# Rounding converted weights on GpSimd, with a shorter warm-up and a new instruction order, in attention with a feed-forward block

## The chip, the core and the metric

The kernel runs on one core of a Trainium2 chip. The metric is the device time of one execution in microseconds (us). The core has five engines with one instruction queue each: TensorE (PE; its weight loads are shown as PEld), VectorE (DVE), ScalarE (ACT), GpSimd (POOL) and SyncE (SP, which here only starts transfers). Instructions of one queue start in order; an instruction waits until those of other engines that it depends on have signalled.

## What is computed

Eight batches of eight heads; queries are averaged in pairs, so 1152 keys meet 576 queries of 64 dimensions. Attention's result goes through a feed-forward block whose hidden value is the largest of three products. All in 32-bit floats.

```python
q_pool = q.reshape(B, H, S // 2, 2, D).mean(axis=3)
scores = scale * np.matmul(q_pool, k.transpose(0, 1, 3, 2))
scores = scores - np.max(scores, axis=-1, keepdims=True)
attn = np.exp(scores)
attn = attn / (np.sum(attn, axis=-1, keepdims=True) + 1e-09)
x = np.matmul(attn, v)            # then heads side by side: 4608 tokens x 512
h = np.maximum(np.maximum(x @ w1, x @ w2), x @ w3)   # 512 -> 768
return h @ w_out                                     # 768 -> 512
```

## The kernel before

**Units.** The work is cut into 64 units: a batch (8), a pair of heads (4), one half of the queries (288). Unit d computes scores for nine blocks of 128 keys (`scores`, lines 570 to 770) and the values (`values`, lines 773 to 981). Each score block is a product of rounded keys with the high and the low half of the queries (L592, L593, tile pqk, two buffers); ScalarE copies it out of PSUM (L605, tile s), VectorE keeps a running maximum (L611, L614, tile acc). The maximum over keys is spread (L646 to L688) and subtracted (L739: on VectorE, for one head of the first 8 units on GpSimd), ScalarE takes exponentials (L745), GpSimd or TensorE adds over keys (ksum L762, L764; psum L870), and TensorE multiplies by the values (pav L786). A score tile is free again only when the value product and the key sum of the unit have read it.

**Two halves of a number.** TensorE is fed with rounded numbers (F32R). So a 32-bit operand is split: the high half is the rounded copy, the low half the difference. Queries and keys are split that way (heads after the first: L473, L477, L480, L484), x (L942, L945), the hidden value h (L1151, L1154) and the weights.

**The first pair of heads** has code of its own (`first_heads`, lines 363 to 442). Its keys come in three blocks c of 384 columns per head; ScalarE rounds a block (L402) and VectorE (block 0) or GpSimd (blocks 1 and 2) makes the low half (L407). While the first transfers run, TensorE is kept busy by a warm-up of products on ones: 6 steps of 1920 columns, 36 matmuls of 288 columns (L350, list WARM).

**The weights.** They arrive as 64-bit floats. For batch 0, `convert` (lines 993 to 1029) turns 512 columns at a time into 32-bit floats: ScalarE scales both words (L1004, L1012), VectorE shifts (L1007), GpSimd adds (L1015). `piece` (lines 1031 to 1050) then makes the two halves, in 26 pieces: the high one on ScalarE (L1042), the low one on GpSimd (L1045). `store` writes the finished group of weights (tile w, two buffers, 13 groups) to memory (L1057); batches 1 to 7 only read it back (`fetch`, L1083). The feed-forward products are L1123 (tile ph, three weight matrices) and L1177 (tile po, w_out); their results leave PSUM by ScalarE or VectorE (hm L1141, L1143; ob L1193). They have two PSUM buffers ("ff"). Batch b's feed-forward runs beside the attention units of batch b + 1, the last one alone.

**The order.** Every step names the engines that it may run on with a cost in us, and the steps that it waits for. `arrange` (lines 151 to 244) simulates the engines by these costs and takes, on the engine that is free first, the ready step of the lowest rank; the order that results is written out as it is, queue by queue. A step's rank is mostly its class's entry in RANK (lines 35 to 83; "first_" entries are added for units below 8, ffn, rate and their "0" forms shift feed-forward steps by batch and by place in the batch), plus an entry of TUNE (18 per class, for units 0 to 17). From unit 18 on TUNE gives nothing. Ranks are in the thousands and unit numbers only below 64, so classes stand in the order of their RANK:

```python
return Step(plan, lambda: d + R[ffn] + R[rate] * n * i / 576 + R[key] + tuned(key, d + 8 * i / 576), engines, fn, after, **kw)
```

Here n is 8 and i runs from 0 to 576 within a batch's feed-forward; i is 432 where w_out begins.

Of the kernel before, what the change touches and what calls it, by code (L numbers as in the profile page):

```python
# [22 lines left out]
QH = 288  # L23
# [12 lines left out]
    "qk": -3130.6658,  # L36
    "cp": -1826.0788,
    "mx": -3810.9001,
    "rows": -8627.0757,
    "red": -43.3158,  # L40
    "bc": -3872.8251,
    "sub": 6258.0329,
    "spread": 1085.8561,
    "exp": 2331.9394,
    "keys": 2364.6864,
    "av": -1042.0366,
    "xcopy": -3440.4973,
    "psum": 3883.7886,
    "sums": -2422.2708,
    "inv": 2073.6634,  # L50
    "xm": -7068.4991,
    "load": -380.5043,
    "prep": 2642.0348,
    "move": 4629.5675,
    "split": 2839.5003,
    "ffn": 3762.7022,
    "ffn0": -465.7092,
    "rate": 35.7318,
    "mm": 2092.8736,
    "fetch": -2282.852,  # L60
    "evac": -3702.58,
    "hhigh": -1168.7886,
    "hlow": -5067.5631,
    "conv": -1572.4688,
    "rate0": 690.1207,
    "first_qk": -4407.8227,
    "first_cp": -1651.3185,
    "first_mx": -1346.0576,
    "first_sub": -2911.0325,
    "first_exp": -3297.3165,  # L70
    "first_keys": -289.0476,
    "first_av": 2482.2468,
    "first_xcopy": -3190.556,
    "first_psum": -1205.5463,
    "first_sums": -2967.258,
    "away": 2349.2695,
    "first_inv": 1449.6935,
    "first_xm": 6167.6523,
    "first_load": 2699.3536,
    "first_prep": -2816.0705,  # L80
    "first_move": 5356.3819,
    "first_split": 50.1713,
# [6 lines left out]
    "rows": [-175.81, -2924.97, -2232.22, -1314.67, 460.97, -3131.21, -418.16, -775.77, 2638.05, -927.09, 854.38, -786.06, 870.99, 708.38, -1156.9, 783.78, -1226.45, -1786.97],  # L89
    "red": [-2241.91, -542.05, 2974.71, 1758.28, -503.57, -1328.97, -782.7, 268.29, -512.53, 1720.33, -786.63, 1917.46, -1276.72, -581.32, 1526.87, -982.28, 184.37, -1249.52],  # L90
    "bc": [-664.57, 172.69, 2235.21, -9.63, -2441.8, -729.01, -812.33, 1298.95, -879.37, 2407.08, -662.96, 602.59, -2313.96, -5.85, -833.79, -753.42, 1381.1, 1053.26],
    "sub": [1288.35, -514.25, -1250.29, 867.55, -2087.59, 292.93, 318.27, -1814.19, 1210.45, 2668.87, 2171.77, 369.02, -1898.63, 935.45, -1626.68, -3948.77, 760.75, 1293.88],
    "spread": [-3017.17, -782.21, 146.5, -2338.72, 283.85, 375.19, 1264.03, -184.45, 2476.42, -589.85, -889.16, -2121.58, -406, -365.93, -385, 222.06, 1726.42, -33.34],
    "exp": [-1955.85, 4048.31, 465.95, -1397.74, 2172.54, 57.59, 651.46, 1134.86, -2438.63, 651.63, 813.75, -394.37, -1502.34, -93.57, 128.48, -687.9, -1912.66, -882.69],
    "keys": [1293.35, 536.44, -1206.73, -2762.49, 299.9, -744.66, -1425.81, -1312.24, 2139, -1917.58, -1157.75, 956.01, -1910.32, 1738.77, 1666.71, -1147.47, 1393.11, 254.81],
    "av": [-46.8, -2772.09, 336.08, 254.7, -2006.33, 1355.89, -3050.17, 1140.74, 218.38, -1842.44, 1293.07, 1165.55, 1669.17, -2607.14, -3030.98, -265.36, 1892.55, -473.41],
    "xcopy": [1417.03, 3211.46, -2262.39, 1303.49, 1208.8, -1718.5, -1526.9, -1467.75, 1451.2, -291.98, -438.62, 1058.33, 24.62, -517.18, 2377.34, -1577.76, 1437.68, 1053.33],
    "psum": [-2696.17, 1357.23, 1123.89, -4598.94, -144.12, 2609.44, -634.47, -2662.38, 1500.72, 1846.17, 111.17, -1242.53, -742.72, 989.9, 116.69, 160.62, -1251.54, 5420.26],
    "sums": [755.08, -874.34, 2205.9, 1188.61, 2102.95, 1489.15, 888.5, 2924.58, -884.62, 329.82, 2011.77, 1627.77, -2594.78, 42.45, -415.63, 733.21, 998.28, 1272.22],
    "inv": [463.45, 1.26, -506.82, 1133.91, -722.58, 827.13, 992.35, 5572.02, 3655.18, -2791.21, 1439.12, -1477.71, -3129.81, 262.16, 1885.92, -1076, 735.07, 1310.17],  # L100
    "xm": [250.61, 363.42, 1361.26, -1104.64, 147.92, -2589.27, 2273.74, 1215.79, 575.43, -427.34, -352.49, -2255.54, -399.51, 1677.21, -584.59, -1147.25, -244.86, -131.38],
    "load": [2580.7, -865.03, -2039.98, -671.65, -1758.9, 899.44, -899.78, -2532.24, 591.45, -1279.02, -1811.66, -1149.59, -471.31, -2359.87, 747.59, 1478.6, 781.71, 3443.62],
    "prep": [476.96, 26, 434.64, 281.83, -1092.64, -1322.6, 197.4, 1715.5, -1576.39, -2069.68, 777.66, 2379.06, 2668.96, 973.44, -514.25, -545.63, 217.96, 1502.65],
    "move": [-2126.63, 2238.79, 2678.63, 569.66, 1278.92, -1444.12, -2083.36, 1728.83, 846.71, -399.4, -501.92, 120.68, -383.26, 2378.59, 559.61, 1007.33, -1306.78, -1660.5],
    "split": [-1015.88, -1480.7, 1498.66, -186.59, 1691.42, -889.06, 512.38, -1694.37, -1338.11, 333.89, -1295.44, -2899.8, -2636.37, 4383.83, 550.6, -2444.64, 241.3, 116.47],
    "mm": [-115.23, 683.46, 280.54, 2090.93, -498.08, -510.9, 1188.76, 1536.93, 1257.07, 486.25, 402.45, -1117.45, -2060.38, -1143.13, 652.06, -1654.27, 259.36, -1950.85],
# [27 lines left out]
WARM = [288] * 6  # L134
APART = 0
SWITCH = 0.3
WIRE = 0.4


class Step:  # L140
    def __init__(self, plan, urgency, engines, fn, after, tail=0.0, take=None, give=None, cols=0, mode=0, size=0):
        self.size = size
        self.urgency, self.engines, self.fn = urgency, engines, fn
        self.tail, self.take, self.give, self.cols, self.mode = tail, take, give, cols, mode
        self.index = len(plan)
        self.after = [a for a in after if a is not None]
# [100 lines left out]
def pe(n):  # L247
    return ("pe", n * 1e-3)
# [15 lines left out]
def tile_attention_ffn(  # L264
# [11 lines left out]
    nc = tc.nc  # L276
# [75 lines left out]
    x = None  # L352
# [634 lines left out]
    def ffn(b, cs, d):  # L987
# [117 lines left out]
        n = 0  # L1105
# [163 lines left out]
```

## Time and profile before

| | us |
|---|---|
| median of 3 runs | 1326.4 (1324.9 to 1326.55) |
| profiled execution, its own time | 1328.54 |
| span of that execution, first to last instruction | 1326.8 |
| TensorE busy | 1292.6 (97%) |
| VectorE busy | 996.9 (75%) |
| ScalarE busy | 985.3 (74%) |
| GpSimd busy | 1054.7 (79%) |
| mean granted clock of TensorE | 0.987 of full |

How to read it: busy times add up the instructions of an engine and overlap with those of others. TensorE's matmuls are pipelined and the ends of their records are modelled, so a matmul of 288 columns has a record of about 0.3 us while one starts every 0.13 us; a TensorE that looks busy may still have small gaps. The chain of waits is the one path of work that ended last, followed back from the end: at each step to what released it. What is on the chain set the time; what is not was hidden. A releaser is inferred from signals.

### The profile page before, as it was taken

The numbers are of one execution on the slowest core, as the hardware profiler recorded it, in microseconds if no ns is written. First come the engines' busy times: TensorE is split into PE (matmuls) and PEld (weight loads), VectorE is DVE, ScalarE is ACT, GpSimd is POOL, SyncE is SP. The second block draws the span as 40 slices with busy tenths as digits, with TensorE's granted clock in tenths as the row PEclk, the third lists the DMA queues.
The fourth block names the chain that finished last, engine by engine and source line by source line (L and its number), as shares of the span: only waits on it lengthen the run. The fifth ranks groups of instructions, "written<-read, shape, count | busy, mean of one in ns | idle before, by whom it ended". The sixth has DMA issues, their size and how long they took to land.

```text
span 1326.8 us, 26771 instructions
## 1 busy us (share of the span) xinstructions
PE 1292.6 (97%) x9732; PEld 1114.3 (84%) x9732; DVE 996.9 (75%) x1601; ACT 985.3 (74%) x1889; POOL 1054.7 (79%) x869
## 2 busy tenths in 40 slices
PE   7989999999999999999999999999999999999999
PEld 6545687878888998888899888888898888888998
DVE  5676699798788878788788888888788878885110
ACT  5887799899877887778877787777777787775211
POOL 5686576889999798988988998888988899878210
PEclk6899999999999999999999999999999999999999
DMA  5765566886776677656776667566776757642544
GB/s 161 221 174 140 144 216 191 248 251 187 220 217 185 217 221 212 188 163 193 210 232 185 199 204 221 174 202 177 225 216 173 227 156 236 208 126 80 182 161 158
DMA packets 107795, 255.39 MB, mean 192 GB/s; under 512 B 14608, under 2 KB 78608, under 8 KB 98448
## 3 DMA queue, kind: packets, MB, share of 16 engines
q1 hardware_dynamic: 107376, 253.09, 63.8%
q8 instruction: 78, 1.28, 0.4%
q10 hardware_dynamic: 288, 0.59, 0.1%
q14 instruction: 53, 0.43, 0.1%
HBM read 158.47 MB, written 22.02 MB: 136 GB/s over the span
## 4 chain that ended last, share of the span: by engine, by line
PE 77%; ACT 9%; DVE 5%; DMA 5%; POOL 1%; issue 1%; SPq 1%; ACTq 0%; DVEq 0%; POOLq 0%
PE ph L1123 28%; PE pav L786 18%; PE pqk L592 10%; PE po L1177 10%; PE pqk L593 9%; ACT s L745 3%; ACT s L605 3%; DMA w<-w_split 2%; DVE s L739 2%; DVE acc L614 2%; PE psum L870 2%; DMA qq<-qraw 1%; ACT kraw L480 1%; DMA kraw<-in_kT_dram 1%; POOL ksum L764 1%
## 5 line engine op out<-in xcount | busy, mean ns | idle before, releaser
L764 POOL TENSOR_TENSOR ksum<-ksum,s 128x576 f32<-128x576 f32 x360 | 518.1, 1443 | 10.6 <-ACT s L745 1.2
L1123 PE MATMUL ph<-xh,w 128*128 128x288 f32 x2304 | 512.1, 296 | 2.8 <-DMA w<-w_split 1.9
L605 ACT COPY s<-pqk 128x576 f32<-128x576 f32 x576 | 365.1, 640 | 101.6 <-PE pqk L593 95.6
L614 DVE TENSOR_TENSOR acc<-acc,pqk 128x576 f32<-128x576 f32 x448 | 333.8, 745 | 113.6 <-ACT s L605 109.5
L1123 PEld LDWEIGHTS ph<-xh,w 128*128 128x128 f32 x2304 | 388.1, 189 | 5.0 <-issue 1.9
L745 ACT ACTIVATE s<-s 128x864 f32<-128x864 f32 x384 | 352.4, 934 | 50.2 <-DVE s L739 46.6
L592 PE MATMUL pqk<-qq,kc 128*128 128x288 f32 x1152 | 338.4, 310 | 25.6 <-DVE acc L614 17.1
L1123 PE MATMUL ph<-xl,w 128*128 128x288 f32 x1152 | 339.6, 295 | 0.0
L593 PE MATMUL pqk<-qq,kc 128*128 128x288 f32 x1152 | 324.7, 298 | 0.0
L786 PE MATMUL pav<-s,v 128*64 128x288 f32 x2304 | 293.1, 410 | 0.8 <-DVE s L739 0.8
L592 PEld LDWEIGHTS pqk<-qq,kc 128*128 128x128 f32 x1152 | 220.5, 191 | 68.8 <-DVE acc L614 30.4
L786 PEld LDWEIGHTS pav<-s,v 128*64 128x64 f32 x2304 | 161.1, 137 | 116.4 <-issue 10.8
L593 PEld LDWEIGHTS pqk<-qq,kc 128*128 128x128 f32 x1152 | 221.4, 192 | 0.0
L739 DVE TENSOR_TENSOR s<-s,spare 128x864 f32<-128x864 f32 x216 | 220.0, 1042 | 1.0
L1123 PEld LDWEIGHTS ph<-xl,w 128*128 128x128 f32 x1152 | 217.4, 189 | 0.0
L1177 PE MATMUL po<-h,w 128*128 128x288 f32 x1152 | 169.2, 295 | 0.1
L1177 PEld LDWEIGHTS po<-h,w 128*128 128x128 f32 x1152 | 158.2, 188 | 0.8 <-issue 0.7
L739 DVE TENSOR_TENSOR s<-s,pmb 128x864 f32<-128x864 f32 x144 | 148.3, 1043 | 0.8
L1143 DVE TENSOR_TENSOR hm<-hm,ph 128x288 f32<-128x288 f32 x192 | 85.0, 443 | 71.3 <-PE ph L1123 70.2
L1154 POOL TENSOR_TENSOR h<-hm,h 128x288 fp32r<-128x288 f32 x96 | 77.2, 811 | 75.5 <-ACT h L1151 75.2
L484 POOL TENSOR_TENSOR kraw<-kraw 128x1152 fp32r<-128x1152 f32 x31 | 83.1, 2681 | 37.5 <-ACT kraw L480 35.3
L762 POOL TENSOR_TENSOR ksum<-s 128x576 f32<-128x576 f32 x56 | 81.9, 1462 | 31.1 <-ACT s L745 27.3
(62 smaller groups left out, 1037.1 us busy)
## 6 DMA issues: line engine op xcount, KB each, us to landing
w<-w_split SPq DMA_DIRECT2D x63, 1024.0 KB, 6.1
kc<-kraw SPq DMA_DIRECT2D x372, 96.0 KB, 3.5
qq<-qraw SPq DMA_DIRECT2D x248, 144.0 KB, 3.8
w<-w_split SPq DMA_DIRECT2D x28, 768.0 KB, 4.6
v<-in_vr_dram SPq DMA_DIRECT2D x32, 576.0 KB, 4.4
kraw<-in_kT_dram SPq DMA_DIRECT2D x31, 576.0 KB, 4.5
qraw<-in_qT_dram SPq DMA_DIRECT2D x31, 576.0 KB, 4.9
w<-in_win_dram SPq DMA_DIRECT2D x18, 512.0 KB, 5.8
```

What stands on the lines that cost most here:

```text
L484: vec[e].tensor_tensor(lo.bitcast(F32R), lo, o.hl[:, 0, x:y], op=ALU.subtract)
L592: nc.tensor.matmul(ps[:, h - hs[0], :QH], w, qq[:, 0, h], start=True, stop=False)
L593: nc.tensor.matmul(ps[:, h - hs[0], :QH], w, qq[:, 1, h], start=False, stop=True)
L605: nc.scalar.copy(o.s[kk // 3][:, kk % 3, slice(*hs)], o.ps[kk, hs][:, :, :QH])
L614: nc.vector.tensor_tensor(acc, acc, ps, op=ALU.max)
L739: vec[e].tensor_tensor(s, s, o.pb[h][:, None, :QH].broadcast_to([P, 3, QH]), op=ALU.subtract)
L745: nc.scalar.activation(s, s, AF.Exp, scale=SCALE)
L764: vec[e].tensor_tensor(o.ksum, o.ksum, x, op=ALU.add)
L786: nc.tensor.matmul(o.pav[64 * h : 64 * h + 64, :QH], pr.v[:, kk, h], o.s[kk // 3][:, kk % 3, h], start=(kk == 0), stop=(kk == NK - 1),)
L1123: nc.tensor.matmul(t.ps[:, :QH], w[:, a, kk], xx[:, kk, qs], start=(kk == 0 and i == 0), stop=(kk == 3 and i == 2),)
L1143: nc.vector.tensor_tensor(part[c], part[c], t.ps[:, :QH], op=ALU.max)
L1177: nc.tensor.matmul(t.ps[:, :QH], w[:, k : k + P], hh[:, kk, qs], start=(kk == 0 and i == 0), stop=(kk == 5 and i == 2),)
```

## The change

Four things. (1) In `piece`, the high half of the converted weights is written by GpSimd (tensor_copy) instead of ScalarE (copy); the planner's cost for it changes from 0.05 + n/985 on ScalarE to 0.145 + n/1000 on GpSimd. GpSimd now does three steps on a piece in a row: the add, the rounding, the difference. (2) The low half of key block 1 of the first pair is made by VectorE instead of GpSimd (block 2 stays on GpSimd). (3) The warm-up is 5 steps instead of 6, 30 matmuls instead of 36. (4) All entries of RANK and all 27 lists of TUNE have new values, so that the planner writes out another order. A new list EXTRA could repeat products of a unit; it is empty.

```diff
 RANK = {
-    "qk": -3130.6658,
+    "qk": -2868.3069,
...
-    "exp": 2331.9394,
+    "exp": 2376.6433,
...
-    "av": -1042.0366,
+    "av": -1904.6789,
...
-    "ffn": 3762.7022,
+    "ffn": 3976.603,
-    "rate": 35.7318,
+    "rate": 202.1667,
-    "mm": 2092.8736,
+    "mm": 1455.0729,
-    "evac": -3702.58,
-    "hhigh": -1168.7886,
+    "evac": -2933.2831,
+    "hhigh": -1829.3266,
...
-    "first_cp": -1651.3185,
-    "first_sub": -2911.0325,
+    "first_cp": -2955.6383,
+    "first_sub": -4009.8304,
...
 TUNE = {
...
-    "conv": [-775.23, -685.78, -579.5, 539.53, 2183.75, 897.35, 545.02, -2095.03, 407.58, 134.55, -762.27, 1076.97, 368.52, 421.44, -190.38, -1005.27, -224.29, -4199.41],
+    "conv": [-809.96, -1110.99, -469.22, 88.55, 1301.21, 1501.32, 973.63, -2464.84, 38.87, -110.1, -474.98, 1024.01, 648.13, 906.91, -240.33, -658.08, -1016.42, -4191.22],
...
-WARM = [288] * 6
+WARM = [288] * 5
+EXTRA = []
...
-                y = step("prep", at, [(pool if c else dve)(n)], lambda e, hs=hs: k_low(e, c, hs), [x])
+                y = step("prep", at, [(pool if c > 1 else dve)(n)], lambda e, hs=hs: k_low(e, c, hs), [x])
...
+        more = EXTRA[d] if d < len(EXTRA) else 0
...
+                        if h < more:
+                            nc.tensor.matmul(ps[:, h - hs[0], :QH], w, qq[:, 0, h], start=True, stop=True)
...
-                nc.scalar.copy(view(0), o.ff[:, x : x + n])
+                nc.gpsimd.tensor_copy(view(0), o.ff[:, x : x + n])
...
-            c = o.step([("act", 0.05 + n / 985)], high, [o.joined] + (wuse[g - 2] if g > 1 else []))
+            c = o.step([("pool", 0.145 + n / 1000)], high, [o.joined] + (wuse[g - 2] if g > 1 else []))
```

## Rows read from the trace of the kernel before

**Rows 1.** The page's busy times: engine, busy us, share, instructions.
```profile
PE 1292.6 (97%) x9732; PEld 1114.3 (84%) x9732; DVE 996.9 (75%) x1601; ACT 985.3 (74%) x1889; POOL 1054.7 (79%) x869
```

**Rows 2.** Stages: length, busy us of each engine (instructions), clock, DMA share, GB/s.
```profile
0.00:160.00 160.00, 140.64 (x950) 90.65 (x952) 104.83 (x181) 121.94 (x211) 105.15 (x77) 0.89 0.59 165
160.00:360.00 200.00, 195.19 (x1514) 161.82 (x1509) 173.53 (x286) 178.13 (x327) 163.06 (x134) 1.00 0.75 222
360.00:1200.00 840.00, 834.97 (x6360) 744.83 (x6359) 690.89 (x1083) 653.30 (x1275) 747.47 (x618) 1.00 0.66 197
```

**Rows 3.** Chain by line: 0-360, 255-305, 305-360, 360-1200 us.
```profile
by line: PE pav L786 13.0%; PE pqk L592 10.2%; ACT s L745 9.1%; ACT s L605 8.2%; PE ph L1123 7.3%; PE pqk L593 7.1%; PE psum L870 6.4%; DVE acc L614 5.6%; DVE s L739 5.5%; issue 3.9%; PE po L1177 3.3%; PE warm L350 1.9%; ACT w L1042 1.5%; D
by line: ACT s L605 20.2%; ACT s L745 18.6%; DVE s L739 13.8%; ACT w_m L1004 6.0%; DVE acc L614 5.8%; ACT w L1042 5.0%; ACT w L1012 4.7%; issue 4.6%; DVE w L1007 3.1%; ACT kraw L480 2.1%; PE pqk L592 2.0%; ACT tops L675 1.7%; PE ph L1123 1.
by line: PE po L1177 21.7%; ACT s L745 13.9%; PE pqk L592 8.5%; PE pav L786 8.3%; PE pqk L593 7.2%; DVE acc L614 6.7%; DVE s L739 6.2%; issue 5.2%; ACT s L605 5.0%; ACT kraw L480 1.9%; ACT w L1042 1.9%; ACT xr L795 1.8%; DVE w L1007 1.3%; A
by line: PE ph L1123 33.8%; PE pav L786 21.1%; PE pqk L592 11.4%; PE pqk L593 10.8%; PE po L1177 9.9%; DMA w<-w_split 2.2%; ACT s L745 1.1%; DMA kraw<-in_kT_dram 1.0%; DVE s L739 1.0%; POOL ksum L764 0.8%; DMA qq<-qraw 0.8%; DMA kc<-kraw 0.
```

**Rows 4.** Groups, TensorE, 160-360 us: count | busy us, mean ns | idle before.
```profile
L870 PE MATMUL psum<-s,ones 128*32 128x288 f32 x128 | 9.4, 412 | 0.0
L870 PE MATMUL psum<-ksum,ones 128*32 128x288 f32 x32 | 5.2, 406 | 0.0
```

**Rows 5.** Chain in order of time: start us, length, engine, tile, line.
```profile
11.35 1.82 POOL kc L407
...
170.75 0.68 ACT w L1042
171.50 1.34 POOL w L1045
...
253.34 1.58 PE psum L870 x20
```

**Rows 6.** Busy time by engine, 255 to 305 and 305 to 360 us.
```profile
255.00:305.00 50.00, 48.28 (x372) 40.78 (x373) 46.70 (x80) 45.79 (x83) 39.74 (x33) 1.00 0.76 223
305.00:360.00 55.00, 53.29 (x402) 44.67 (x401) 44.48 (x70) 49.04 (x95) 53.70 (x47) 1.00 0.74 225
```

**Rows 7.** Line 1042: count, min/median/max ns, first and last start us.
```profile
L1042 ACT CAST w<-w x26: 414/673/724, 49.0 to 349.6; 128x512 fp32r<-128x512 f32 x22, 128x256 fp32r<-128x256 f32 x4
```

**Rows 8.** Instructions of the start: start, length, engine, line, tile, count.
```profile
1.38 0.88 POOL L303 TENSOR_TENSOR share<-ident 128x32 f32<-128x32 f32 x4
...
1.73 6.87 PE L350 MATMUL warm<-warm_w 128*128 128x288 f32 x36 [1.73 <-DVE warm_w L343]
...
8.12 0.56 DVE L407 TENSOR_TENSOR kc<-kraw,kc 64x384 fp32r<-64x384 f32 x1
...
8.73 0.40 PE L592 MATMUL pqk<-qq,kc 128*128 128x288 f32 x1
...
10.51 0.75 DVE L611 TENSOR_TENSOR acc<-s,pqk 128x576 f32<-128x576 f32 x1 [1.83 <-ACT s L605]
...
28.92 2.03 POOL L739 TENSOR_TENSOR s<-s,pmb 128x864 f32<-128x864 f32 x1
```

**Rows 9.** The granted clock (column PEclk) at 12 to 16 us, TensorE alone.
```profile
12.00:14.00 2.00, 0.79 (x3) 0.68 0.00 0
14.00:16.00 2.00, 1.50 (x7) 0.50 0.15 14
```

**Rows 10.** Waits, 160-360 us: who for whom, total us, times, longest.
```profile
POOL w L1045 <- ACT w L1042: 9.6, 4, 7.0
...
ACT w L1042 <- POOL w L1015: 1.4, 1, 1.4
...
DVE w L1007 <- POOL w L1045: 0.7, 1, 0.7
```

**Rows 11.** TensorE's longest wait in 0 to 160 us.
```profile
PEld pqk L592 <- DVE acc L614: 20.8, 26, 2.2
```

**Rows 12.** The exponentials, 360 to 1200 us.
```profile
L745 ACT ACTIVATE s<-s 128x864 f32<-128x864 f32 x264 | 242.5, 933 | 43.5 <-DVE s L739 41.2
```

More of the change, by code (lines that the diff above doesn't have):

```diff
@@ L35 @@
 RANK = {
-    "qk": -3130.6658,
[L37 to L43, printed above, removed]
-    "exp": 2331.9394,
-    "keys": 2364.6864,
-    "av": -1042.0366,
[L47 to L55, printed above, removed]
-    "ffn": 3762.7022,
@@ L76 @@
[L76 to L82, printed above, removed]
+    "qk": -2868.3069,
+    "cp": -2134.0238,
+    "mx": -3748.5895,
+    "rows": -8216.3872,
+    "red": -296.425,
+    "bc": -3190.1383,
+    "sub": 6075.1265,
+    "spread": 2389.0945,
+    "exp": 2376.6433,
+    "keys": 2673.6741,
+    "av": -1904.6789,
+    "xcopy": -3619.5103,
+    "psum": 4076.3279,
@@ new lines @@
+    "sums": -2770.5084,
+    "inv": 2031.4121,
+    "xm": -6756.9391,
+    "load": -2078.8382,
+    "prep": 2559.7192,
+    "move": 4497.1853,
+    "split": 2687.3376,
+    "ffn": 3976.603,
+    "ffn0": -948.7583,
+    "rate": 202.1667,
+    "mm": 1455.0729,
+    "fetch": -1618.5505,
+    "evac": -2933.2831,
+    "hhigh": -1829.3266,
+    "hlow": -5510.6917,
+    "conv": -1459.2673,
+    "rate0": 325.0053,
+    "first_qk": -4697.6199,
+    "first_cp": -2955.6383,
+    "first_mx": -871.2094,
+    "first_sub": -4009.8304,
@@ L83 @@
+    "first_exp": -3336.7665,
+    "first_keys": -488.2755,
+    "first_av": 2766.7179,
+    "first_xcopy": -3290.2382,
+    "first_psum": -681.4404,
+    "first_sums": -2704.2618,
+    "away": 2677.5829,
+    "first_inv": 1046.8111,
+    "first_xm": 6611.8451,
+    "first_load": 2548.2234,
+    "first_prep": -2792.2189,
+    "first_move": 5305.1274,
+    "first_split": -265.9161,
 }
@@ new lines @@
+    "rows": [-795.77, -3949.51, -2995.24, -1731.16, -236.89, -3026.16, -379.59, 78.98, 3138.03, -1797.54, 317.54, -770.9, 1665.85, 56.59, -1711.41, 1144.69, -281.8, -2780.22],
+    "red": [-2059.12, -1315.9, 3004.3, 2032.55, -748.45, -1778.05, -329, 519.15, -758.74, 2028.43, -953.73, 2257.57, -1402.81, -205.63, 1164.21, -1619.35, -241.11, -1340.23],
+    "bc": [-660.04, 379.5, 2219.87, 152.41, -2679.29, -145.77, 428.08, 1565.46, -863.73, 3133.39, -1493.42, 285.1, -2186.24, 441.31, -332.12, -841.44, 862.97, 1136.06],
@@ new lines @@
+    "sub": [1697.51, -425.9, -659.39, 669.55, -2174.08, 892.38, 1196.17, -1204.52, 1637.44, 5155.38, 2337.42, 261.9, -2492.66, 765.8, -2072.7, -3941.66, 1287.22, 1175.25],
+    "spread": [-1999.32, -1641.56, 909.39, -1749.7, 1207.32, 579.57, 1554.11, -200.53, 2015.85, -110.33, -504.63, -2254.48, -692.54, 0.3, -743.05, 154.73, 1692.13, -486.29],
+    "exp": [-813.86, 4169.89, 116.1, -1295.46, 1852.66, -187.04, 942, 1213.32, -2414.08, 829.64, 1437.25, 354.18, -1637.61, 144.02, -795.32, 687.19, -2838.87, -493.57],
@@ new lines @@
+    "keys": [1609.75, 988.68, -918.47, -2790.06, 450.14, -617.36, -1716.64, -1154.03, 2951.69, -1608.43, -1037.38, 1693.16, -2215.35, 1866.19, 1363.02, -1803.21, 2466.35, 440.98],
+    "av": [474.56, -2381.13, -192.31, 776.91, -2699.41, 2230.95, -2948, 2527.62, -104.12, -1783.51, 1044.14, 2433.32, 2413.85, -2738.64, -2297.97, -333.68, 1994.64, -988.13],
+    "xcopy": [1341.75, 2738.51, -2784.17, 977.79, 1376.35, -1248.86, -1673.03, -2211.07, 1735.43, -168.4, -1566.77, 792.8, -99.62, -763.46, 2214.04, -2834.6, 1813.55, 901.32],
@@ new lines @@
+    "psum": [-2599.25, 2102.01, 2013.28, -4903.61, -861.2, 2202.61, -784.16, -3267.42, 1477.1, 1116.18, -116.18, -1242.68, -283.89, 532.73, 146.55, 493.81, -2331.15, 6172.34],
+    "sums": [1945.99, -1054.47, 1519, 1915.89, 2933.29, 2244.91, 2241.61, 2334.55, -979.22, -224.2, 2299.73, 1593.74, -2683.02, 413.51, -267.04, 1376.63, 1634.31, 1105.3],
+    "inv": [-71.08, 636.45, 82.09, 1088.23, -540.77, 852.48, 1946.06, 7100.67, 4197.81, -3946.08, 1551.28, -942.94, -3084.13, 1044.76, 1606.68, -1457.52, 1420.68, 1359.83],
@@ L620, in scores @@
                     r,
-                    [pe(266 * n)],
+                    [pe(266 * n + 132 * more)],
                     product,
                     pr.kready[kk // 3] + pr.qready[o.half] + ([chain.get(d - 4)] if apart else uses[-2]) + [last[0]],
-                    cols=576 * n,
+                    cols=576 * n + 288 * more,
                     take="ff" if apart else None,
```

47 lines of the change are left out of this document (11 added, 36 removed), and 6 rows, old and new, of the table TUNE.

## Prediction

> **What bounds the kernel now.** I read the busy times first. TensorE is busy for 97% of the span, the other engines for 74 to 79% [rows 1]. That alone would make TensorE the bound everywhere, so I cut the span into stages [rows 2]. From 360 to 1200 us TensorE is busy in 835 of 840 us, and the chain of work there runs through its matmuls (ph, pav, pqk, po: 87% together) [rows 2, 3]. Nothing that other engines save can show in that stage; 5 us of idle time is all there is to gain. From 0 to 160 us TensorE is busy in 140.6 us, a part of it at half clock, and 19 us are plainly idle. From 160 to 360 us it looks full (195 of 200), but matmul ends are modelled, so I count. Of the 1514 matmuls, 160 are narrow sums that pass at 1.58 us per 20 [rows 4, 5] and 16 are tiny. The other 1338 at the steady pace (840 us / 6360 = 0.132 us [rows 2]) need 177 us; with 13 us for the sums that is 190, so some 10 us of this stage are lost. The same count in 255 to 360 us (774 matmuls [rows 6], the sums in about the same proportion) gives some 98 of 105 us: 7 us lost there.
>
> Who loses them is told by the chain. From 255 to 305 us it runs almost without TensorE: ScalarE's score copies, exponentials and weight steps and VectorE's subtractions carry it, and the rounding of the upper half (w L1042) alone is 5.0% of those 50 us, 2.5 us; from 305 to 360 us it is 1.9% of 55, 1.0 us; over 0 to 360 us it is 1.5%, 5.4 us [rows 3]. So the line that is moved does lie on the path, but only in the stage where batch 0's weights are converted.
>
> **The change, part by part.**
>
> The rounding leaves ScalarE. It is 26 casts, 22 of 512 columns at about 0.67 us and 4 of 256 at 0.41 to 0.45, the last at 349.6 us [rows 7]. That is 16.5 us of ScalarE work, none of it after 350 us. On the chain it is 5.4 us. One piece of that (170.75, 0.68 us) goes on into GpSimd's subtraction of the same weights [rows 5], so there the cast is only replaced by another; 4.7 us are left. What is late next is VectorE: in 255 to 305 us it is busy 46.7 of 50 us against ScalarE's 45.8 [rows 6], so it has 3.3 us to give, which covers the 2.5 us of that stretch but not much more. I take 4.0 us as the gain, with 0 and 7 (TensorE's loss after 255 us) as ends.
>
> It lands on GpSimd. No f32 copy with rounding by this engine is in the trace, so I bound it. Above: the subtraction on the same 512 columns, 1.34 us [rows 5], which reads two operands. Below: the fixed part of any such instruction. Four 32-column sums take 0.88 us, 0.22 each, and 864 columns take 2.03 us [rows 8], so 2.2 ns a column and some 0.15 us fixed. A copy reads one operand where these read two; half of 2.2 ns gives 0.15 + 0.56 = 0.7 us for 512 columns and 0.43 for 256. I take 0.7, midway between the ends, since the operands read are the one thing in which it differs. That adds 22 x 0.7 + 4 x 0.43 = 17 us to GpSimd. The Trainium skill ("GPSIMD Engine Reference", section 4.1) calls two-input elementwise work there about twice as slow as on VectorE but one-input work roughly line-rate; at its 1.2 GHz the 512 columns would be an estimated 0.43 us and the addition 10 us, and the sum below would stay as it is.
>
> Whether GpSimd can take it: from 255 to 305 us it is busy 39.7 of 50 us, from 305 to 360 us 53.7 of 55 [rows 6]. Also, it loses four waits for this cast, 9.6 us in 160 to 360 us; the waits of ScalarE and VectorE for its weight steps come to 2.1 us in the same 200 us [rows 10]. So up to 305 us the copies are hidden by its idle time. In the last stretch 3 x 0.7 + 4 x 0.43 = 3.8 us meet 1.3 us of room: it falls 2.5 us behind, and at the upper bound of 1.34 (0.71 for the small ones, by the slope above) 5.6 us. It has time to catch up (747 of 840 us busy afterwards [rows 2]) and no wait for its key sums shows, so I price this at nothing in the sum and keep it as a rival. The new wait is that GpSimd, not ScalarE, now waits for TensorE to release the weight buffer, with key sums and query parts queued behind; at 164 to 171 us it stood idle for 7.0 us on this already [rows 10], so it costs nothing new.
>
> The second key block's low half goes from GpSimd to VectorE. GpSimd needs 1.82 us for it, from 11.35 us, and TensorE's next products wait until it ends at 13.2 (11.35 + 1.82) [rows 5]. VectorE does half as many columns (384) in 0.56 us and 576 of another sum in 0.75, so 1 ns a column [rows 8]: 768 columns take 0.56 + 0.38 = 0.94. VectorE is free at 11.26 (10.51 + 0.75), so the block is ready at about 12.3: 0.85 us earlier. The running maximum that stood at 11.8 moves back by half a microsecond; the products that need its buffer come only after those now released. Behind it the chain passes mostly through TensorE, ScalarE and VectorE (neither a transfer nor GpSimd is among its larger lines up to 360 us [rows 3]), so I let 0.8 us reach the end, with 0 and 1 as bounds. GpSimd's third block also starts earlier.
>
> The warm-up loses six of 36 matmuls, about 0.7 us off its end at 8.6 us [rows 8]. The first product's second half waits for its keys' low half until 8.68 us anyway (8.12 + 0.56), and starts at 8.73 [rows 8]. Gain 0 to 0.1, taken as 0. The clock might fall earlier: now the granted clock is 0.68 of full in 12 to 14 us and 0.50 after, the lower of the two levels [rows 9], after TensorE stood idle for want of that key block. If the first eight products came at the lower level they would take twice the steady pace and cost 8 x 0.13 = 1.1 us. The empty list EXTRA adds no instruction.
>
> The order is replanned by new ranks everywhere. For units from 18 on the tuning lists do not apply, so ranks can be compared by hand: on TensorE the classes keep their order (qk, av, then the feed-forward matmuls), and on ScalarE rounding h now comes ahead of the exponentials. For earlier units the lists shift single steps by thousands and cannot be read; this part has no row. I put 0 in the likeliest sum and price it both ways below.
>
> Sum: 4.0 + 0.8 = 4.8 us off. The profiled execution took 1328.5 us, so it would be 1323.7; the median shown, 1326.4, lies 2.1 lower, so 1321.6.
>
> **The rivals.**
>
> Replanning helps the first stage. In 0 to 160 us TensorE waits 20.8 us for the running maximum (VectorE), 26 times [rows 11]. Ranks there change most. If a third of it goes, 7 us, on top of the 4.8: 1314.6. For it: no engine is full there (ScalarE 122, VectorE 105, GpSimd 105 of 160 us [rows 2]). Against it: the units follow one another through a chain that an order can shift but not shorten.
>
> The gain ends at the next limit. VectorE takes ScalarE's place at once, and TensorE fills the gaps with matmuls that it needs anyway; only the 0.8 us are left: 1325.6. VectorE's 46.7 of 50 us speaks for it. That the clock takes back the start's gain belongs here too: 1322.7 with all else kept. On the clock the Trainium skill ("TensorE: Matmul & The Clock Gate", part 1) says that the throttled state is the default and activity releases it; by that a shorter warm-up is a risk, and no row here shows the start with fewer matmuls.
>
> GpSimd becomes the bound in 305 to 360 us. If its copies cost near 1.34 us, 5.6 us of backlog delay the output weights and the score buffers; it decides from the point at which a copy costs over about 0.9 us and the backlog exceeds what was gained: 1326.4 - 0.8 + 5.6 = 1331.2 if ScalarE's relief then buys nothing. Against it: the few waits for GpSimd.
>
> Slower by the order (the other side): feed-forward evacuations behind exponentials. By the ranks for late units, evac was 60 to 346 over a batch and stood ahead of exp (2332); now it runs from 1043 to 2661 and crosses exp (2377) at 82% of the batch, within the output matmuls. Five or six of 8 output evacuations of a batch then queue behind exponentials, 0.93 us apiece [rows 12], in batches 2 to 6: 28 x 0.93 = 26 us if TensorE waited each time. It has two buffers there, so it waits only if several exponentials come first; at one time in three 8.7 us: 1321.6 + 8.7 = 1330.3.
>
> **How the numbers follow.** Forecast (4.8 off, give or take 2) 0.43; replanning helps the first stage 0.22; gain ends at the next limit 0.15; GpSimd bound 0.07; evacuations late 0.13. A measurement of this kernel can tell about 0.2%, 2.7 us, from no change: faster means below 1323.7. Faster: 0.36 of the forecast's 0.43 and all of the second, 0.58. Same: the rest of the forecast, the third case and a little of the last two, 0.24. Slower: 0.18. The range is 1312 to 1331: below, the second rival with the upper end of ScalarE's relief; above, the late evacuations; only a full GpSimd limit or a worse order lies beyond.
>
> **What would show it.** ScalarE's busy time 16 us lower and GpSimd's 10 to 30 higher; a copy row on GpSimd at 0.45 to 0.9 us; the first product on the second key block at about 12.4 us instead of 13.2; TensorE's stage from 360 us on at the same pace, and reached 4 to 5 us earlier. Wrong would be: waits for GpSimd's sums or weights in 300 to 360 us, more TensorE idle time after 360 us, or a first stage whose length changes by more than 2 us, which would mean that the order and not the cast sets the result.

## The result: 10.6 us faster, two thirds of it in the first 160 us, where only 4 of the 26 moved casts lie

The changed kernel takes 1315.9 us (median of 4 runs, 1313.7 to 1317.6) against 1326.5 us for the kernel before measured beside it (4 runs, 1324.9 to 1327.8). The ratio is 0.9918, with a 95% interval from 0.9903 to 0.9932: 0.8% faster. Run again beside the kernel before, it took 1316.6 us, 0.9913 [0.9887, 0.9939]. The forecast was 1321.6 us: right in direction, inside its range, and short by 5.7 us, half of the gain. The time is nearer to that of the rival "replanning helps the first stage" (1314.6 us, chance 0.22) than to the forecast. The profiled execution took 1317.6 us, its span 1315.8.

The busy times of the changed kernel, from its page, and then the answer for the line of the moved cast (line numbers are 1 to 4 higher than before):

```profile
PE 1288.9 (98%) x9726; PEld 1112.9 (85%) x9726; DVE 998.9 (76%) x1602; ACT 972.7 (74%) x1863; POOL 1068.1 (81%) x894
```

```profile
L1046 POOL CAST w<-w x26: 404/660/744, 49.8 to 332.6; 128x512 fp32r<-128x512 f32 x22, 128x256 fp32r<-128x256 f32 x4
```

Against [rows 1] ScalarE has lost 12.6 us (16 was worked out) and GpSimd gained 13.4; the copy takes 0.66 us for 512 columns and 0.40 for 256 [rows 7 for the same casts on ScalarE]. The two sizes of the copy are those that were predicted (0.7 and 0.43). The last copy starts at 332.6 us, where the last cast before started at 349.6.

Where the time went is read from the stages of the changed kernel, the same stretches as [rows 2], and, in a second answer, the two parts of the conversion as in [rows 6]:

```profile
0.00:160.00 160.00, 145.41 (x995) 95.17 (x996) 111.83 (x193) 124.87 (x220) 107.47 (x82) 0.91 0.62 175
160.00:360.00 200.00, 195.93 (x1528) 164.22 (x1528) 175.15 (x288) 168.89 (x308) 179.13 (x160) 1.00 0.76 228
360.00:1200.00 840.00, 835.86 (x6369) 746.50 (x6368) 692.41 (x1086) 651.57 (x1272) 750.82 (x619) 1.00 0.65 195
```

```profile
255.00:305.00 50.00, 48.41 (x377) 39.39 (x377) 43.99 (x75) 42.60 (x80) 44.36 (x44) 1.00 0.70 203
305.00:360.00 55.00, 53.49 (x409) 47.28 (x406) 46.48 (x74) 45.39 (x85) 52.86 (x47) 1.00 0.85 255
```

The stretches are of fixed length, so the number of TensorE's matmuls in each (behind its busy time) says how far the kernel has come. In the first 160 us it issues 995, of which 30 are warm-up: 965 products, where the kernel before issued 950 - 36 = 914. The 51 more are, at the steady 0.132 us, 6.7 us. From 160 to 360 us it issues 1528 against 1514: another 14, 1.8 us. From 360 to 1200 us it issues 6369 against 6360: 9 more, 1.2 us. The first feed-forward product gives the same answer in time; this is its row in the kernel before (start of the first: 162.1 us) and in the changed one (155.2 us):

```profile
L1123 PE MATMUL ph<-xh,w x2304: 290/296/401, 162.1 to 1304.2; 128*128 128x288 f32 x192
```

```profile
L1127 PE MATMUL ph<-xh,w x2304: 290/296/402, 155.2 to 1293.2; 128*128 128x288 f32 x192
```

So 6.9 of some 11 us are won before the first feed-forward product, when 4 of the 26 copies have been made (49.8 to 71.9 us). What TensorE waits for in the first 160 us has the same name as in [rows 11], and less of it (total us, times, longest):

```profile
PEld pqk L596 <- DVE acc L618: 15.6, 22, 1.6
```

That is 5.2 us less than the 20.8 before. (Whether the whole 6.9 us are the order's is taken up in the last section: the granted clock differs too.) The start itself, in the changed kernel's timeline (start, length, engine, line, tile, count, idle time before):

```profile
1.74 6.67 PE L351 MATMUL warm<-warm_w 128*128 128x288 f32 x30 [1.74 <-DVE warm_w L344]
...
11.18 0.95 DVE L408 TENSOR_TENSOR kc<-kraw,kc 64x768 fp32r<-64x768 f32 x1
12.29 0.37 PE L596 MATMUL pqk<-qq,kc 128*128 128x288 f32 x1 [1.61 <-DVE kc L408]
12.50 1.83 POOL L408 TENSOR_TENSOR kc<-kraw,kc 64x768 fp32r<-64x768 f32 x1 [10.24 <-ACT kc L403]
```

The key block takes VectorE 0.95 us (worked out: 0.94) and TensorE goes on at 12.29 us (worked out: about 12.3 to 12.4).

And the chain of work from 255 to 305 us, as in [rows 3], now in the changed kernel:

```profile
by line: POOL ksum L768 11.2%; DMA qraw<-in_qT_dram 10.5%; PE pav L790 9.1%; DMA w<-in_wout_dram 9.0%; PE ph L1127 8.5%; issue 8.2%; ACT s L609 7.7%; ACT s L749 6.6%; POOL w L1049 5.3%; POOL w L1019 4.0%; POOL xr L805 3.3%; ACT xh L946 2.8%
```

ScalarE's score copies and exponentials have fallen from 39% to 14% of it. What took their place is not VectorE, as I had said, but GpSimd's key sums and weight steps and two transfers (the first began at 251.4 us, so most of its 10.5% lies ahead of the stretch). The repeat's chain agrees: of the 50 us VectorE has 1.1, GpSimd 12.7, transfers 4.7.

### The profile page after: what moved, and what is told of

Read it like the earlier page. It is cut to its first block, busy times and chain, and to the rows that moved or that the text cites. A ratio compares the mean times of both kernels' runs of the same rounds, so it can differ in the third digit from the quotient of the medians.

```text
span 1315.8 us, 26773 instructions
## 1 busy us (share of the span) xinstructions
PE 1288.9 (98%) x9726; PEld 1112.9 (85%) x9726; DVE 998.9 (76%) x1602; ACT 972.7 (74%) x1863; POOL 1068.1 (81%) x894
## 4 chain that ended last, share of the span: by engine, by line
PE 81%; DMA 7%; ACT 5%; POOL 3%; DVE 2%; issue 1%; SPq 1%; ACTq 0%; DVEq 0%; POOLq 0%
PE ph L1127 31%; PE pav L790 20%; PE pqk L596 10%; PE pqk L597 9%; PE po L1181 8%; DMA w<-w_split 3%; PE psum L874 2%; ACT s L609 2%; DMA qq<-qraw 2%; ACT s L749 1%; DMA kraw<-in_kT_dram 1%; DVE acc L618 1%; POOL ksum L768 1%; SPq L519 1%; DMA w<-in_win_dram 1%
## 5 line engine op out<-in xcount | busy, mean ns | idle before, releaser
L596 PEld LDWEIGHTS pqk<-qq,kc 128*128 128x128 f32 x1152 | 220.1, 191 | 56.7 <-DVE acc L618 20.5
```

The lines of the kernel that those rows point to most:

```text
L596: nc.tensor.matmul(ps[:, h - hs[0], :QH], w, qq[:, 0, h], start=True, stop=False)
```

## Experiments

The change has a written order (the planner's, from ranks and costs) and three parts (the move, the key block, the warm-up). The first question is how much each carries. In the kernels called "order kept" the order of the instructions is that of the kernel they start from: only the engine that an instruction runs on, or a count, is changed, and the planner is not told. In the others it replans. The table has every run; products are TensorE's matmuls without the warm-up, by 160 us, from 160 to 360 and from 360 to 1200.

| kernel | by 160 | 160-360 | 360-1200 | median us | ratio to before [95%] |
|---|---|---|---|---|---|
| before | 914 | 1514 | 6360 | 1326.5 to 1328.1 | 1 |
| changed | 965 | 1528 | 6369 | 1315.9 | 0.9918 [0.9903, 0.9932] |
| changed, again (c3) | 985 | 1518 | 6367 | 1316.6 | 0.9913 [0.9887, 0.9939] |
| a1 before + move | 912 | 1499 | 6361 | 1333.4 | 1.0040 [1.0026, 1.0054] |
| a2 before + three parts | 910 | 1488 | 6346 | 1331.7 | 1.0031 [1.0018, 1.0045] |
| d1 before + 18 of 26 casts moved | 903 | 1495 | 6338 | 1333.6 | 1.0045 [1.0033, 1.0057] |
| b1 changed, move undone | 974 | 1501 | 6384 | 1318.4 | 0.9923 [0.9899, 0.9947] |
| b2 changed, key block undone | 981 | 1524 | 6378 | 1315.8 | 0.9900 [0.9876, 0.9924] |
| b3 changed, warm-up undone | 965 | 1530 | 6382 | 1315.0 | 0.9890 [0.9861, 0.9919] |
| b4 changed, all three undone | 965 | 1496 | 6387 | 1318.9 | 0.9923 [0.9900, 0.9947] |
| a3 before + new ranks, replanned | 956 | 1441 | 6316 | 1341.5 | 1.0100 [1.0073, 1.0127] |
| a4 changed + old ranks, replanned | 894 | 1404 | 6204 | 1364.9 | 1.0281 [1.0258, 1.0305] |
| c1 before + new ranks of units 0 to 7, replanned | 902 | 1374 | 6362 | 1346.5 | 1.0133 [1.0104, 1.0163] |
| d2 changed + evacuations early, replanned | 977 | 1530 | 6267 | 1334.8 | 1.0045 [1.0023, 1.0066] |

### The order against the parts

**b4: the new order with the old parts** (order kept).

```diff
-        for _ in range(1920 // n):
+        for _ in range(1920 // n if i < 4 else 2 * (1920 // n)):
...
-            vec[e].tensor_tensor(lo, ...)
+            (nc.gpsimd if c == 1 else vec[e]).tensor_tensor(lo, ...)
...
-                nc.gpsimd.tensor_copy(view(0), o.ff[:, x : x + n])
+                nc.scalar.copy(view(0), o.ff[:, x : x + n])
```

> The changed kernel's written order with all three parts undone: casts on ScalarE, key block 1 on GpSimd, 36 warm-up matmuls. With the kernel before, the changed kernel and the three parts in the old order (0.3% slower) this fills the table of order by parts. Order theory: 1317 to 1319, first feed-forward product of batch 0 at 156 to 157 us. Fit theory: 1321 to 1327: the first stage's 6 us are there, and the stage to 355 us gives most of them back.

Measured: 1318.9 us, 0.9923. The first feed-forward product comes at 155.2 us, the same as in the changed kernel. So the gain up to there needs none of the three parts. In all, b4 is 9.3 us below the kernel before measured beside it (1328.1), while b2 and b3, in the same session and with the cast on GpSimd, are 12.3 and 13.1 below. By that share the order alone gives some 8 of the 10.6 us. Its first two stages:

```profile
0.00:160.00 160.00, 145.31 (x1001) 95.53 (x1002) 110.85 (x192) 126.99 (x224) 106.92 (x79) 0.93 0.63 175
160.00:360.00 200.00, 193.83 (x1496) 160.49 (x1496) 171.74 (x279) 176.29 (x322) 163.96 (x134) 1.00 0.75 222
```

The order's gain doesn't lie in the first stage alone. From 160 to 360 us b4 issues 18 products fewer than the kernel before, a loss of 2.4 us, and from 360 to 1200 us 27 more, a gain of 3.6. The table has this late gain in all six traces of the new order (6367 to 6387 products against 6338 to 6361 in the four of the old). TensorE's wait for the running maximum from 360 to 1200 us goes the same way: 4.2 to 5.7 us in the four of the old order, 1.5 at most in the six of the new. These are the kernel before and the changed one:

```profile
PEld pqk L592 <- DVE acc L614: 4.2, 6, 1.4
```

```profile
PEld pqk L596 <- DVE acc L618: 1.5, 2, 0.8
```

**a2: the three parts in the old order** (order kept), the opposite corner.

```diff
-        for _ in range(1920 // n):
+        for _ in range(1920 // n if i < 5 else 0):
...
-            vec[e].tensor_tensor(lo, ...)
+            (nc.vector if c == 1 else vec[e]).tensor_tensor(lo, ...)
...
-                nc.scalar.copy(view(0), o.ff[:, x : x + n])
+                nc.gpsimd.tensor_copy(view(0), o.ff[:, x : x + n])
```

> The kernel before, its order kept, with all three changed parts: the casts on GpSimd, the low half of key block 1 on VectorE, five warm-up steps instead of six. Parts theory: 4.8 us less, about 1321.6, nearly half of the measured gain. Order theory: only the start's 0.8 to 1.5 us, about 1325. If this reaches 1316 the new order did nothing.

Measured: 1331.7 us, 1.0031: slower than before by 4.5 us. The same three edits that were to bring 4.8 us cost nearly as much, as long as the order is the old one.

**b1, b2, b3: one part undone in the new order** (order kept). The diffs are the three pieces of b4's, one at a time.

> The changed kernel, its written order kept, with the 26 casts back on ScalarE at the places where GpSimd had them. Theory 'order and move fit each other' (alone each was slower): 4 to 9 us above the changed kernel's 1316, so 1320 to 1325, lost between 155 and 355 us, where ScalarE now has 12 us more; the first stage (first feed-forward product at 155 us) unchanged within 1 us. Theory 'the order is everything': within 2 us of 1316.

> The changed kernel, its order kept, with the low half of key block 1 back on GpSimd. If the 0.8 us at the start reaches the end: first unit's maximum 0.8 us later and the end as much later, about 1316.7. If it is lost on the way, as it was in the old order by unit 4: no difference. If the clock falls earlier because TensorE idles longer there: up to 3 us more.

> The changed kernel, its order kept, with 36 warm-up matmuls instead of 30. If the sixth step only filled time: first products at the same time within 0.2 us, total within 1 us of 1316. If the shorter warm-up let the first products start earlier: 0.5 us more. If the longer one holds the clock better at the start: less.

Measured beside b4 and the same runs of the kernel before: 1318.4, 1315.8 and 1315.0 us. The two with the cast on ScalarE (b1, b4) lie at 0.9923, the two with it on GpSimd at 0.9900 and 0.9890. That is 3.2 us between the means. The intervals overlap, but the single runs, all of one session, don't: the eight with the cast on ScalarE lie between 1317.7 and 1320.4 us, the eight with it on GpSimd between 1312.7 and 1317.2. The traces say the same: from 160 to 360 us the kernels of the new order issue 1496 and 1501 products with the cast on ScalarE and 1518 to 1530 with it on GpSimd, 1525 on average, so the move brings 26 products, 3.5 us, in that stage. Key block and warm-up bring nothing that reaches the end. At the first unit's maximum b2 and b3 are 1.0 and 0.8 us behind the changed kernel's first run. b3 is level two units later. b2 has to be read beside the repeat, whose clock ran as b2's did: there 0.6 us of the 1.0 are left at 119 us, 0.4 at 220, and none at 240.

What the move takes away in the new order is one wait; this is b1's, from 160 to 360 us:

```profile
POOL w L1049 <- ACT w L1046: 19.1, 12, 7.0
```

GpSimd stands for 19.1 us, 12 times, waiting for a ScalarE that makes the cast late; with the copy on its own queue this wait doesn't exist (before, in the old order: 9.6 us, 4 times [rows 10]). That this wait is what costs the 3.5 us is argued from its size and place; no run removes the wait alone.

### Why the same move costs 5 us in the old order

**a1: the move alone in the old order** (order kept).

```diff
-                nc.scalar.copy(view(0), o.ff[:, x : x + n])
+                nc.gpsimd.tensor_copy(view(0), o.ff[:, x : x + n])
```

> The kernel before with one line changed: the high half of the converted weights is written by GpSimd at the place in the written order where ScalarE had it; the planner still counts it as ScalarE's, so every queue keeps its order but for these 26 casts. If the relief of ScalarE is what pays (the forecast's largest term), 4 us less than before, about 1322. If the new order pays, no difference of more than 1 us, 1325 to 1327. If GpSimd is too full in 305 to 360 us, 2 to 6 us more.

Measured: 1333.4 us, 1.0040. Its profiled execution was the fastest of ten (1329.5 us), so the trace holds only some 2.3 us of the loss by 360 us, in two places. I call lag the time by which a unit's maximum comes later than the same unit's in the kernel before. The first place, 229 to 237 us, GpSimd and ScalarE in the kernel before, then in a1 (timeline):

```profile
229.87 1.34 POOL L1045 TENSOR_TENSOR w<-w,w 128x512 fp32r<-128x512 f32 x1
231.14 0.82 POOL L1154 TENSOR_TENSOR h<-hm,h 128x288 fp32r<-128x288 f32 x1
231.89 1.44 POOL L470 TENSOR_TENSOR qraw<-qraw 128x576 f32<-128x576 f32 x1
...
233.37 0.67 ACT L473 CAST qraw<-qraw 128x576 fp32r<-128x576 f32 x1 [0.25 <-POOL qraw L470]
234.07 0.21 ACT L675 COPY tops<-tops 64x18 f32<-64x18 f32 x1
```

```profile
228.07 1.27 POOL L1042 CAST w<-w 128x512 fp32r<-128x512 f32 x2
...
233.32 1.44 POOL L470 TENSOR_TENSOR qraw<-qraw 128x576 f32<-128x576 f32 x1
...
234.79 0.67 ACT L473 CAST qraw<-qraw 128x576 fp32r<-128x576 f32 x1 [1.40 <-POOL qraw L470]
235.49 0.20 ACT L675 COPY tops<-tops 64x18 f32<-64x18 f32 x1
```

Two copies, 1.27 us, now stand in GpSimd's queue ahead of the query parts (L470), which end 1.4 us later. ScalarE takes its steps in order, so it waits 1.40 us instead of 0.25 for them, and the maximum's copy (L675) that VectorE, the next scores and TensorE depend on starts 1.4 us later. The next unit's maximum ends 1.1 us behind the kernel before, up from 0.1 to 0.3 in the units before. In a2 and d1, which make the same two copies there, the same step stands idle for 1.39 and 1.35 us. Their answers name a key transfer as what released it, but in both, as in a1, the step starts 0.03 us after GpSimd's query parts end. In a1 half of this is made good by 309 us (lag 0.6); in a2 and d1 the lag grows by 1.8 and 1.5 us up to 257 us and stays. In the changed kernel no wait of ScalarE for these query parts is listed between 160 and 360 us.

The second place is the end of the conversion, 335 to 366 us. The chain there in the kernel before, then in a1, and a1's busy times from 305 to 360 us:

```profile
by line: ACT s L745 24.6%; PE ph L1123 12.0%; PE po L1177 9.0%; ACT s L605 8.9%; PE pqk L592 8.6%; PE pqk L593 7.7%; issue 3.8%; DVE s L739 3.4%; ACT kraw L480 3.4%; ACT w L1042 3.3%; DVE acc L614 2.5%; DVE w L1007 2.3%; ACT w_m L1004 2.2%;
```

```profile
by line: POOL ksum L764 22.8%; POOL w L1045 13.1%; issue 10.3%; POOL kraw L484 8.4%; PE ph L1123 7.7%; POOL w L1015 6.4%; POOL w L1042 6.4%; PE pqk L592 5.5%; POOL ksum L762 4.6%; POOL qraw L477 4.5%; PE pqk L593 4.3%; PE po L1177 3.9%; DVE
```

```profile
305.00:360.00 55.00, 52.09 (x389) 43.05 (x389) 43.98 (x70) 45.94 (x87) 54.68 (x53) 1.00 0.68 209
```

GpSimd is busy 54.68 of 55 us and the chain has passed to it from ScalarE, whose exponentials (24.6%) led it before. New waits for it stand in a1's answer for the same stretch (waiter, releaser, total, times, longest):

```profile
DVE ks L809 <- POOL ksum L764: 1.6, 1, 1.6
PEld po L1177 <- POOL w L1045: 1.4, 2, 0.7
```

The lag grows here from 0.8 us at 344 us to 2.3 at 366, and in a2 from 2.9 to 4.5. This is the third rival, GpSimd as the bound of 305 to 360 us, at a copy of 0.66 us, well under the 0.9 from which I had let it decide.

**d1: only the casts of the input weights moved, old order** (order kept): the last eight, of the output weights, stay on ScalarE.

```diff
-                nc.scalar.copy(view(0), o.ff[:, x : x + n])
+                (nc.gpsimd.tensor_copy if g < NG // 2 else nc.scalar.copy)(view(0), o.ff[:, x : x + n])
```

> The kernel before, its order kept, with 18 of the 26 casts on GpSimd: those of the input weights, the last at 292 us; the 8 of the output weights, in the stretch where GpSimd has no room, stay on ScalarE. If the full GpSimd in 305 to 360 us is what makes the whole move cost 5 us in the old order: within 2 us of before, and no step of 1 to 2 us at 340 to 363 us against before. If the old order loses by the move anywhere: 3 to 6 us above before, as with all 26.

Measured: 1333.6 us, 1.0045: as slow as a1. The chain from 335 to 366 us goes through a transfer and ScalarE again, not through GpSimd:

```profile
by line: DMA out_dram<-ob 28.1%; ACT s L745 25.4%; ACT s L605 10.7%; PE po L1177 9.0%; PE pqk L592 6.1%; ACT w L1042 5.1%; PE ph L1123 5.1%; PE pqk L593 5.1%; issue 5.1%; DVE s L739 3.4%; ACT kraw L480 3.4%; DVE acc L614 2.5%; DVE w L1007 2
```

and its lag doesn't grow from 344 to 366 us (3.8 us at both). So the step of the second place is gone, and the first remains; yet the median is no better. In its trace 1.3 us of the lag are there before the first converted weight is used (a first stage with granted clock 0.88 instead of 0.89), 1.5 us come up to 257 us, 0.9 up to 344, and 2.5 after 366, of which 1.1 by 383. I can't name all of these. The two places are shown where they occur; that they are the whole loss of the move in the old order is not.

### Ranks, costs and units

**a3: the old parts and costs, new ranks, replanned; a4: the new parts and costs, old ranks, replanned.**

```diff
-RANK = {"qk": -3130.6658, ...    # and TUNE
+RANK = {"qk": -2868.3069, ...    # a3: the changed kernel's; a4: the reverse
```

> The kernel before with the new RANK and TUNE alone; the three parts stay as before and the planner makes its order with the old costs. Order theory: 6 to 9 us less, 1317 to 1320, with the first feed-forward product of batch 0 some 5 us earlier than 162.1 us. Parts theory: within 2 us of before. A third possibility, that ranks and parts only fit each other: slower than before by some us.

> The changed kernel with the old RANK and TUNE, so that the planner makes an order from the old ranks with the new costs. Parts theory: 4 to 5 us less than before. Order theory: 0 to 2 us less. If old ranks fit the old costs only: slower than before.

Measured: 1341.5 and 1364.9 us, 1.0100 and 1.0281. Both are far slower than either whole kernel. a3 has the early gain (first feed-forward product at 156.3 us) and loses it and more behind it. Its first two stages:

```profile
0.00:160.00 160.00, 144.08 (x992) 95.26 (x993) 109.22 (x191) 126.09 (x223) 106.85 (x79) 0.91 0.62 174
160.00:360.00 200.00, 189.15 (x1441) 154.64 (x1440) 167.63 (x273) 172.01 (x312) 157.57 (x129) 0.99 0.72 211
```

73 products fewer than before from 160 to 360 us are 9.6 us, and 44 fewer from 360 to 1200 another 5.8. The order that comes out of a mixture is neither of the two. I take it that ranks and costs were fitted to each other; nothing here shows how they were found. So these two runs don't say what the ranks are worth; only the kernels whose order is kept do.

**c1: the new ranks for the first eight units only, replanned from the kernel before.**

```diff
-    "qk": [1176.06, 259.57, -1247.88, 879.02, 4169.33, 1040.87, 253.82, -902, -819.57, ...
+    "qk": [909.48, 186.31, -1912.19, 113.27, 3831.42, 420.74, 1499.73, -424.72, -819.57, ...
```

(and so for the other classes, so that rank plus list entry is the changed kernel's for units 0 to 7 and the old one behind).

> The kernel before; only the steps of units 0 to 7 get the ranks that they have in the changed kernel, everything later and all three parts are as before, and the planner makes its order from that. If the first stage's gain lies in the ranks of those units: first feed-forward product of batch 0 at 155 to 157 us instead of 162.1 and, where nothing later falls out of step, 1319 to 1322 in all. If it falls out of step as the new ranks alone did: 1325 to 1340 with the same early start. If the ranks of the steps after unit 7 make the gain: product at 161 us or later.

Measured: 1346.5 us, 1.0133, and the first feed-forward product at 167.3 us, 5.2 later than before. So the first eight units' ranks alone, planned with the old costs, don't give the early gain, while all ranks with the old costs (a3) do; what in the order makes it is not narrowed down further.

**d2: evacuations ahead of exponentials, replanned from the changed kernel**, the rival on late evacuations turned round: if output evacuations that queue behind exponentials cost time, an earlier rank should win it.

```diff
-    "evac": -2933.2831,
+    "evac": -4933.2831,
...
-    "evac": [..., -340.45, 470.29, ..., 157.94, -1552.05],
+    "evac": [..., 1659.55, 2470.29, ..., 2157.94, 447.95],
```

(the lists of units 8 to 17 are raised by as much, so that the change bears on the later units).

> The changed kernel with the rank of feed-forward evacuations lowered by 2000 from batch 1 on, so that they stand ahead of exponentials as they did before; batch 0's are as in the changed kernel. If evacuations queued behind exponentials cost something in the late stage: 2 to 4 us less than the changed kernel (TensorE's wait for the output copies gone). If they are hidden and only the written order shifts: within 2 us. If the shift puts other steps out of line: some us more.

Measured: 1334.8 us, 1.0045: 18 us slower than the changed kernel. It is not behind it up to 360 us and then falls behind, by some 9 of the 18 us between 600 and 800 us. The steady stage and the two waits of TensorE's weight loads that have grown there (360 to 1190 us):

```profile
360.00:1200.00 840.00, 827.61 (x6267) 735.38 (x6265) 680.64 (x1064) 643.15 (x1251) 735.38 (x608) 0.99 0.65 193
```

```profile
PEld pav L790 <- DVE s L743: 8.1, 5, 2.3
...
PEld pqk L596 <- DVE acc L618: 5.3, 5, 2.1
```

In the changed kernel the second of these is 1.5 us, the first isn't in the list, and the wait that the late evacuations cause is in it with 2.8 us:

```profile
PEld po L1181 <- ACT ob L1197: 2.8, 4, 1.1
```

That wait is gone in d2, and 102 products, 13.5 us, with it. But d2 is replanned, as a3, a4 and c1 are, and all four are slower than the kernel before. So the 18 us are the price of the whole order that came out; what early evacuations cost by themselves is not shown.

**c3: the changed kernel again**, for the spread.

> The changed kernel once more, unaltered, for a direct comparison with the three others and to see how far two profiled executions of one program differ by stage: 1314 to 1318, the first feed-forward product within 2 us of 155.2.

Measured: 1316.6 us, 0.9913. Its trace stands in the last section.

## Why the prediction was right, and where it was not

The direction and the range held, but in good part by luck: of the 10.6 us, what the forecast priced accounts for some 3, and with the order left as it was the same three parts make the kernel slower (a2). The rest came from the term that the sum had at 0.

**"I put 0 in the likeliest sum" (the order): the term that was mis-sized.** Without the three parts it brings some 8 us (b4). I had the right row for it: TensorE's 20.8 us of waiting for the running maximum [rows 11], no engine full in that stage, and the rival took a third of that wait, 7 us. Measured are 6.9 us for the stage, and that wait is 5.2 us shorter; the clock may have a share in the 6.9 (last section). What spoke against it, that a chain can be shifted but not shortened by an order, did not hold. My explanation is that steps of different units stand in the same in-order queues, so that the order sets how long a step of the chain stands behind one that isn't; which steps these are is not shown. The forecast also counted nothing behind 360 us, though it had seen 5 us of idle time there: the order gains in that stage too (1.2 us in the changed kernel, 3.6 in b4). And one reading of the ranks was wrong, though no term hung on it: rounding h runs from 2147 to 3765 over a batch, so it stands ahead of the exponentials (2377) only in the first 14% of it. A part of the change that can't be read step by step isn't a part worth nothing, and the forecast had given it nothing.

**"4.0 us as the gain" (ScalarE's relief): right only within the new order.** There the move brings 3.5 us in the conversion stage (b1, b4 against the rest), of which some 3 arrive at the end. In the old order, for which I had worked it out, it brings nothing and costs 5 to 6 us (a1: 1333.4 against 1327.2). The step that failed there is "up to 305 us the copies are hidden by its idle time". GpSimd's 39.7 busy of 50 us [rows 6] is the mean of 255 to 305 us; at 228 to 239 us it has no gap, and the copies push the query parts that ScalarE waits for. Also failed: "What is late next is VectorE". Of the chain from 255 to 305 us GpSimd has 14.5 us beside VectorE's 10.7 in a1 and 14.3 beside 16.2 in a2, and in the changed kernel 15.0 beside 0.8; before it had none.

**"0.8 us reach the end" (key block): 0.** The block was priced rightly (0.95 us against 0.94) and the start is as early as worked out. But undoing it (b2) leaves 1315.8 us. My reason, that no transfer and no GpSimd step is among the chain's larger lines up to 360 us, was read from the kernel before; in the changed kernel's chain from 0 to 360 us the query transfer has 4.2%. A chain that waits on a transfer, whose time doesn't come earlier, gives no early start through; that this is what takes the 0.8 us was not tested.

**Warm-up 0: right.** b3 differs by nothing (1315.0 beside b2's 1315.8). The "about 0.7 us off its end" is 0.2 in the two traces (8.4 against 8.6 us), because the granted clock rose later in the changed kernel's (at 7.2 us against 5.9), so that 22 of its warm-up matmuls stand some 0.24 us apart, against 16 before. It fell to its lower level at 14.0 us instead of 12.7, but that isn't the shorter warm-up's doing: over the fourteen traces it falls between 12.0 and 14.7 us with 36 matmuls and between 12.0 and 14.2 with 30. From the rule of the Trainium skill ("TensorE: Matmul & The Clock Gate", part 1) that activity releases the throttle I had seen a risk in a shorter warm-up; between 30 and 36 matmuls these runs show none.

**The price of GpSimd's copy, 0.7 and 0.43 us: right** (0.66 and 0.40). The nearest rows, half a two-operand step and a fixed part, gave it; the Trainium skill's "roughly line-rate" ("GPSIMD Engine Reference", section 4.1), taken as an estimated 0.43 us for 512 columns, is too low by a third without a fixed part, and right in setting one-input work apart: the two-operand subtraction beside it takes 1.3 us.

**GpSimd as the bound (0.07): real in the old order, without a loss in the new.** In a1 and a2 the chain of 335 to 366 us runs through it. In the changed kernel it is busy 52.9 of 55 us from 305 to 360, less than the 53.7 before [rows 6] though the copies are now on it; its last copy starts at 332.6 us. It still has 20.6 us of the chain of those 55 in the first trace, but none in the repeat's, and TensorE issues as many products there as before (409 and 403 against 402).

**Late evacuations (0.13, +8.7 us): the mechanism is there, its size was not.** TensorE's output matmuls wait for them 2.8 us from 360 us on. The factor that failed is "at one time in three": 2.8 us are about a ninth of the 26.

**The sum.** 4.8 was forecast for three parts; in the new order they give some 3, all from the move. The rest, some 8, is the term at 0. The case was foreseen among the signs: a first stage that changes by more than 2 us "would mean that the order and not the cast sets the result".

## What to carry to other kernels

Where every engine takes its instructions in a written order, an edit and the order are one change: price the edit against the queue at the place where it lands (what stands behind it there, and who waits for that), not against the engine's idle share of a stage. The same move was worth -3 us in one order and +5 in another, and replanning with half of the fitted numbers lost 1 to 3%. A replanned order needs a term of its own, bounded by the waits of the stages that no engine fills; zero is a choice like any other.

## What the hardware showed that I had not expected

The first stage of one and the same program differed between its two profiled executions by more than its end did. These are the stages of the changed kernel's repeat, to be read beside the first run's above:

```profile
0.00:160.00 160.00, 145.89 (x1015) 96.82 (x1016) 114.31 (x197) 126.82 (x223) 107.48 (x82) 0.94 0.63 176
160.00:360.00 200.00, 195.26 (x1518) 163.03 (x1517) 174.14 (x285) 167.99 (x306) 180.31 (x160) 1.00 0.77 228
```

The granted clock is 0.94 in the mean of the first 160 us, and 0.91 in the other run: TensorE is at its lower level (1.2 GHz) once, for 20.5 us from 14 us on, and not again, where the other run has two more stretches of 3.4 us, at 51.6 and 72.0 us. The repeat is 20 products, 2.6 us, ahead at 160 us and level at the end. In the kernel before there are four such stretches, 34 us together, and its mean is 0.89. So a part of the first stage's 6.9 us may be clock rather than waits. As an estimate: the repeat has 6.8 us less at the lower level than the changed kernel's first run and is 2.6 us ahead; the first run has 6.8 us less (27.3) than the kernel before, so some 2.6 of the 6.9 us could be clock. The 5.2 us less waiting and the shorter low stretches can't be taken apart here, since no run holds one of them fixed. That the order gains in this stage is not in doubt: the first feed-forward product starts at 162.1 to 163.4 us in the four traces of the old order and at 152.6 to 155.2 in the six of the new.
